# Leaky pass read from PSUM, weight requests on another queue, one conversion step later

## The chip, the cores and the metric

The kernel runs on one core of one Trainium2 chip. The metric is the device time of one execution in microseconds (us); the time before is 1096.64, the median of 3 runs (1096.25 to 1097.05). The engines are named as in the profile: PE multiplies matrices (PEld loads its weights), DVE is the vector engine, ACT the scalar engine, POOL is GpSimd, and SP issues DMAs. Each engine runs its instructions in order, and an instruction that waits holds up all behind it on its engine. "SPq" and "POOLq" are the DMA queues behind requests of SP and GpSimd.

## The reference

Three stages follow each other. First is attention over 4 images of 8 heads with 576 tokens of 64 values, in which every row keeps its 32 largest scores. Second is a dense mixture: 2304 tokens times 512 to 2048 to 512 with a leaky activation in the middle, one slope per hidden column. Third is a mixture of 8 experts, of which each token takes one, if a gate lets it in.

```python
scores = scale * np.matmul(q, k.transpose(0, 1, 3, 2))
kth = np.partition(scores, -32, axis=-1)[..., -32:-31]
scores = np.where(scores >= kth, scores, -1e9)          # then softmax, times v
x = attention.transpose(0, 2, 1, 3).reshape(2304, 512)
h = x @ w_in                                            # 512 -> 2048
g = np.maximum(h, 0.0) + alpha * np.minimum(h, 0.0)
x = g @ w_out                                           # 2048 -> 512
...
h = np.maximum(xc[mask] @ w1[e], 0.0)                   # e: largest gate logit
out[do_compute] = xc + gate_w * (h @ w2[e])
```

## The kernel before

Attention goes block by block: a step is one block of 128 query rows (the last has 64) for a pair of heads. In a step DVE finds the 32 largest scores of each row: a fold by maxima and minima (L438) makes shorter lists, and rounds of MAX8 and MATCH_REPLACE8 (L447, L450) take eight values at a time; L480 then masks the row of 577 scores, ACT takes the exponentials (L472), PE transposes (L510) and multiplies by the values (L543), and DVE scales the product px (L550).

Each step is written out as 14 slots. The table `STEP` says at which slot x each part of the steps around it is issued, and in each slot the planner (`slot`) also issues some of the waiting work of the first mixture, by a cost budget. So the order of instructions on each engine is the order of this program; no engine reorders.

The first mixture works on an image in two parts, of 256 and of 320 token columns; that makes 8 works, each with 16 units `up` (one per 128 hidden columns) and then the output products `down`. Seven of the works lie beside the attention of later steps, in what is called a stretch below; the eighth comes after the attention has ended, in the tail. The numbers are split into a high and a low part in place of full fp32 products, so that a unit has 12 matmuls (L614) into one PSUM bank `pm`, of which the pool has two. After it:

- one slot later, ACT reads the bank twice: relu(h) into `ra` (L625) and relu(-h) into `rb` (L626); the bank is free then (`read()`).
- after `LA` = 4 further slots the unit is ready for DVE's pass ra = -alpha * rb + ra (L638), but in a stretch that pass is held in a list `leaky` until slot 11 (`PH` + 2), so that DVE runs two to four of them just ahead of the next fold.
- ACT copies `ra` into the high part of `g` (L651), and GpSimd's subtraction (`sub`, L108) makes the low part. Late in a step `between` holds this back until slot 1 of the next, since the first GpSimd subtraction after a fold waits until the fold's last DVE pass is done (`gate`).

`need` and `fetch` ask for weights of the first mixture two chunks (1 MB each) ahead; `wload` (L558) puts a request on GpSimd's queue, into one of three buffers `wr`. There are 128 such requests. These weights are in a DRAM scratch: 32 conversions (`convert`) make them beside the first steps from the given weights, each with three ACT passes (L277 to L281), a DVE pass on the bit patterns (`bits`, L285), a split and a store.

SP's queue carries all other loads and stores, among them the value loads of the heads (L369), the rows of the first mixture's result (L764), and the expert weights `wraw` for the last stage (L992). In the tail, `splits` converts the latter on ACT (L998) and on other engines.

Of the kernel before, what the change touches and what calls it, by code (L numbers as in the profile page):

```python
# [7 lines left out]
F32 = mybir.dt.float32  # L8
# [38 lines left out]
LA = 4  # L47
# [11 lines left out]
def kernel(  # L59
# [44 lines left out]
    gate, now, held_back, leaky = [None], [None], [], []  # L104
# [83 lines left out]
    nalpha = const.tile([128, KF], F32, name="nalpha")  # L188
# [27 lines left out]
    def late_loads():  # L216
        nc.sync.dma_start(wg[:, :, :E], w_gate.rearrange("(d p) e -> p d e", p=128))
        nc.sync.dma_start(wg[:, :, E], w_skip.rearrange("(d p) -> p d", p=128))
        nc.sync.dma_start(nalpha, alpha.rearrange("(f p) -> p f", p=128))
# [47 lines left out]
    def convert(i):  # L267
# [37 lines left out]
        return none * (CV - 1) + [bits] + none * (CV - 1) + [split] + none * CV + [store]  # L305
# [274 lines left out]
    def moe1(xx, cols, x2t, base):  # L580
# [18 lines left out]
        hps, held = {}, [0, 0]  # L599

        def hf_of(f):
            return f // fs

        def up(wi, f, sg, half, first):
# [11 lines left out]
            if half == 0:  # L616
                return []
            ra = moe.tile([128, 320], F32, name="ra", tag="ra", bufs=6)[:, 0:n]
            rb = moe.tile([128, 320], F32, name="rb", tag="rb", bufs=4)[:, 0:n]
            held[0] += 1  # L620
            held[1] += 1
# [6 lines left out]
            soon = f >= (hf_of(f) + 1) * fs - 3  # L628

            def late2():  # L630
                if now[0] is None or now[0] > PH + 1 or soon:
                    late3()
                else:
                    leaky.append(late3)

            def late3():
                held[1] -= 1
                nc.vector.scalar_tensor_tensor(ra, rb, nalpha[:, f:f + 1], ra, op0=OP.mult, op1=OP.add)  # L638
                if soon:
                    late4()  # L640
                else:
                    between(late4)

            def late4():
                held[0] -= 1
# [4 lines left out]
                g[f, sg] = gt  # L650
                nc.scalar.activation(gt[:, 0, 0:n], ra, AF.Copy)  # L651
                sub(gt[:, 1, 0:n], ra, gt[:, 0, 0:n].bitcast(F32))
# [34 lines left out]
        for hf in range(nhf):  # L687
            for f in range(hf * fs, (hf + 1) * fs):
                for sg, (c0, c1) in enumerate(cols):
                    for half in range(2):  # L690
                        one = f % 2 == 0 and sg == 0 and half == 0
                        if half == 0:
                            parts.append((lambda: room() and held[0] < 6 and held[1] < 4, None))
# [423 lines left out]
    def main(work, exact, hooks=(lambda: [], lambda: [])):  # L1117
# [138 lines left out]
        for kx in range(-2, K + 2):  # L1256
# [21 lines left out]
            for x in range(NSLOT):  # L1278
# [3 lines left out]
                if x == PH + 2 or now[0] is None:  # L1282
                    late_leaky = leaky[:]
                    leaky.clear()
                else:
                    late_leaky = ()
# [14 lines left out]
                for f in late_leaky:  # L1301
                    f()
                slot(q if kx > -2 or exact else 0.65 if x in (0, 5, 6) else 0.0)
        now[0] = None
        release(leaky)
# [198 lines left out]
```

## Time and profile before

| what | value |
|---|---|
| time, median of 3 | 1096.64 us (1096.25 to 1097.05) |
| the profiled execution, its own time | 1101.48 us |
| its span in the trace | 1099.6 us |
| PE busy | 941.3 us, 86% |
| DVE busy | 938.3 us, 85% |
| ACT busy | 736.3 us, 67% |
| GpSimd busy | 503.5 us, 46% |
| GpSimd's DMA queue (q0) | 138.73 MB, 36.6% of 16 engines' span |
| SP's DMA queue (q1) | 113.62 MB, 32.7% |

A share of busy time is an average over stages with different limits. The rows below are therefore taken by stage: the start (0 to 30 us), the seven stretches (150 to 830), the tail of the first mixture (857 to 930) and the experts after it. The table of stretches lists the engines in the order PE, PEld, DVE, ACT, POOL. The idle time shown for an instruction is that of its engine just before it, with the line that ended it. Where two engines are near their limit, the order of the waits tells more than the busy shares: a wait that is short on one engine can be the one that another waits behind.

### The profile page before, as it was taken

What the parts mean: (1) busy time and instruction counts of PE and PEld (TensorE: products, weight loads), DVE (VectorE), ACT (ScalarE), POOL (GpSimd) and SP (SyncE); (2) the same over time, 40 slices, a digit from 0 to 9 for tenths busy, and PEclk for the clock granted to TensorE, in tenths of its full rate; (3) what the DMA queues carried; (4) which work ended last, traced back from release to release, by engine and by line L of the source; (5) the groups of instructions that cost most, each with busy time, mean ns of one, the idle gap of its engine ahead of it and who ended that gap; (6) DMA issues with size and microseconds to landing.
All of it is one profiled execution on the core that took longest, in us unless ns stands there. A gap on an engine that the chain in (4) does not pass through costs nothing.

```text
span 1099.6 us, 22163 instructions
## 1 busy us (share of the span) xinstructions
PE 941.3 (86%) x7270; PEld 852.3 (78%) x7270; DVE 938.3 (85%) x2943; ACT 736.3 (67%) x1932; POOL 503.5 (46%) x705
## 2 busy tenths in 40 slices
PE   4436659898999898999999899999889799799994
PEld 2235448798998797999988898999789798587883
DVE  4999998999999899899989998998994233899971
ACT  6869858765875685578567767865773352597870
POOL 4866665532662454346335533652452350327220
PEclk9966569998999998999999999999999899899998
DMA  7888985675575566676756577665557897799950
GB/s 229 283 273 213 307 245 184 192 237 171 195 245 189 162 211 220 225 227 207 236 186 189 200 246 221 223 229 181 174 195 243 302 344 261 274 353 396 348 218 14
DMA packets 154284, 254.15 MB, mean 231 GB/s; under 512 B 78062, under 2 KB 110830, under 8 KB 137776
## 3 DMA queue, kind: packets, MB, share of 16 engines
q0 software_dynamic: 20928, 138.73, 36.6%
q1 hardware_dynamic: 132032, 113.62, 32.7%
q8 instruction: 60, 0.98, 0.4%
q14 instruction: 64, 0.52, 0.1%
q10 hardware_dynamic: 1200, 0.30, 0.1%
HBM read 224.20 MB, written 29.71 MB: 231 GB/s over the span
## 4 chain that ended last, share of the span: by engine, by line
PE 45%; DVE 31%; ACT 8%; DMA 7%; issue 5%; POOL 4%; SPq 0%; POOLq 0%; ACTq 0%; DVEq 0%; another core or an unknown queue 0%
PE pm L669 14%; PE pm L614 7%; DVE v L447 6%; DVE F L438 4%; PE px L543 4%; DVE Ex L480 4%; PE px L1045 4%; PE pm L1027 4%; DVE m L438 3%; DVE F L450 3%; DVE ra L638 3%; PE ps L417 3%; PE pt L510 2%; DMA wr<-wout 2%; PE ps L343 1%
## 5 line engine op out<-in xcount | busy, mean ns | idle before, releaser
L614 PE MATMUL pm<-x,wr 128*128 128x256 f32 (+1 forms) x1536 | 246.3, 310 | 14.2 <-DMA wr<-win 6.3
L669 PE MATMUL pm<-g,wr 128*128 128x256 f32 (+1 forms) x1536 | 235.9, 303 | 6.4 <-DMA wr<-wout 6.3
L614 PEld LDWEIGHTS pm<-x,wr 128*128 128x128 f32 x1536 | 216.8, 195 | 21.6 <-issue 8.7
L669 PEld LDWEIGHTS pm<-g,wr 128*128 128x128 f32 x1536 | 210.0, 190 | 12.2 <-issue 4.2
L447 DVE MAX8 v<-F 128x8 f32<-128x72 f32 (+2 forms) x576 | 213.0, 405 | 1.1
L108 POOL TENSOR_TENSOR g<-ra,g 128x256 fp32r<-128x256 f32 (+1 forms) x128 | 108.9, 869 | 119.3 <-DVE st L485 49.6
L480 DVE SCALAR_TENSOR_TENSOR Ex<-sb,v,Ex 128x577 f32<-128x577 f32 x144 | 132.4, 949 | 0.0
L450 DVE MATCH_REPLACE8 F<-v,F 128x72 f32<-128x72 f32 (+1 forms) x432 | 122.9, 290 | 0.0
L422 ACT ACTIVATE sb<-ps 128x288 f32<-128x288 f32 x224 | 80.1, 416 | 63.9 <-PE ps L417 50.3
L472 ACT ACTIVATE Ex<-sb,st 128x576 f32<-128x576 f32 x144 | 105.7, 786 | 0.1
L522 ACT ACTIVATE PT<-pt 128x512 f32<-128x512 f32 x144 | 87.4, 608 | 14.2 <-PE pt L510 13.4
L638 DVE SCALAR_TENSOR_TENSOR ra<-rb,nalpha,ra 128x256 f32<-128x256 f32 (+1 forms) x128 | 71.3, 593 | 29.4 <-ACT rb L626 29.4
L625 ACT ACTIVATE ra<-pm 128x256 f32<-128x256 f32 (+1 forms) x128 | 53.6, 419 | 57.6 <-PE pm L614 55.2
L510 PE MATMUL pt<-ident,Ex 128*128 128x128 f32 x576 | 88.2, 285 | 4.5 <-ACT sb L422 4.3
L543 PE MATMUL px<-PT,vt 128*64 128x128 f32 (+1 forms) x1280 | 90.2, 288 | 0.0
L417 PE MATMUL ps<-kT,qT 64*128 64x288 f32 x576 | 81.2, 355 | 7.6 <-POOL kT L108 2.9
L108 POOL TENSOR_TENSOR x<-xf,x 128x128 fp32r<-128x128 f32 (+1 forms) x80 | 46.7, 584 | 72.0 <-ACT x L552 39.7
L417 PEld LDWEIGHTS ps<-kT,qT 64*128 64x128 f32 x576 | 63.2, 216 | 20.7 <-issue 9.4
L543 PEld LDWEIGHTS px<-PT,vt 128*64 128x64 f32 x1280 | 70.9, 149 | 9.9 <-issue 2.0
L510 PEld LDWEIGHTS pt<-ident,Ex 128*128 128x128 f32 x576 | 72.1, 148 | 7.1 <-ACT sb L422 6.9
L438 DVE TENSOR_TENSOR F<-m 128x144 f32<-128x144 f32 (+2 forms) x240 | 73.0, 356 | 0.0
L651 ACT ACTIVATE g<-ra 128x256 fp32r<-128x256 f32 (+1 forms) x128 | 51.0, 451 | 20.4 <-DVE ra L638 20.4
(434 smaller groups left out, 1975.9 us busy)
## 6 DMA issues: line engine op xcount, KB each, us to landing
wr<-win POOLq DMA_DIRECT2D x64, 1024.0 KB, 6.0
wr<-wout POOLq DMA_DIRECT2D x64, 1024.0 KB, 6.0
wraw<-in_moe_w_dram SPq DMA_DIRECT2D x88, 512.0 KB
wr<-in_moe_w_in_dram SPq DMA_DIRECT2D x16, 512.0 KB
vt<-in_v_dram SPq DMA_DIRECT2D x32, 256.0 KB
win<-cv SPq DMA_DIRECT2D x16, 512.0 KB
wr<-in_moe_w_out_dram SPq DMA_DIRECT2D x16, 512.0 KB
wout<-cv SPq DMA_DIRECT2D x32, 256.0 KB
```

The costliest lines, as they stand in the source:

```text
L108: i = nc.gpsimd.tensor_tensor(o, a, b, op=OP.subtract)
L417: nc.tensor.matmul(self.ps[h, j][:, 0:HALF], lhsT=hd["q"][gp, a, u * 128:(u + 1) * 128], rhs=hd["k"][gp, b_, c0:c0 + HALF], **se)
L438: gate[0] = nc.vector.tensor_tensor(o[:, n_], a[:, n_, 0:w], a[:, n_, w:2 * w], op=op)
L447: nc.vector.max(v8[:, h, r, :], F[:, h, 0:w])
L450: nc.vector.match_replace(out=F[:, h, 0:w], in_to_replace=v8[:, h, r, :], in_values=F[:, h, 0:w], imm_value=NEG)
L472: nc.scalar.activation(self.Ex[:, h, :], self.sb[:, h, :], AF.Exp, bias=self.st[:, 0, h:h + 1], scale=0.125)
L480: nc.vector.scalar_tensor_tensor(self.Exp[:, cs], self.sbp[:, cs], v8[:, h, 3, 7:8], self.Exp[:, cs], op0=OP.is_ge, op1=OP.mult, accum_out ...
L510: nc.tensor.transpose(pt[:, c * 128:(c + 1) * 128], P[:, c0:c0 + 128], ident)
L543: nc.tensor.matmul(x[h * 64:(h + 1) * 64, 0:n], lhsT=hd["vt"][:, h, c, :], rhs=rhs, start=False, stop=(c == SF - 1))
L614: nc.tensor.matmul(hp[:, 0:n], lhsT=w[:, (f % 2) * 8 + a * 4 + d, :], rhs=x[:, d, c0:c1], start=(i == 0), stop=(i == 3 * KD - 1))
L638: nc.vector.scalar_tensor_tensor(ra, rb, nalpha[:, f:f + 1], ra, op0=OP.mult, op1=OP.add)
L669: nc.tensor.matmul(op_[:, 0:n], lhsT=w[:, 2 * f + a, :], rhs=g[(hf + ch) * 8 + f, sg][:, gg, 0:n], start=(i == 0), stop=(i == ni - 1))
```

## The change

The unit's two relu passes become one, relu(-h) into `ra`; the buffer `rb` goes. DVE's pass takes its addend from the PSUM bank: ra = (1 - alpha) * ra + h, with `slope` = 1 - alpha prepared once in place of `nalpha`. The bank is therefore free only when DVE's pass is written (`read()` stands behind it). `LA` goes from 4 to 2, the list `leaky` with its slot 11 is dropped, so that DVE's pass stands wherever its slot comes, and ACT's copy of `g` is issued right behind it; only GpSimd's subtraction still goes through `between`. The limit of four units between relu and pass (`held[1]`) is gone.

`wload` issues its request on SP in place of GpSimd. Of the second conversion (i = 1) `bits` is queued 12 slots after its ACT passes in place of 3, and in the first step slots 3 and 4 get the budget that 5 and 6 had.

```diff
-LA = 4
+LA = 2
...
-        nc.vector.tensor_scalar(nalpha, nalpha, -1.0, None, op0=OP.mult)
+        nc.vector.tensor_scalar(slope, slope, -1.0, 1.0, op0=OP.mult, op1=OP.add)
...
-        return none * (CV - 1) + [bits] + none * (CV - 1) + [split] + none * CV + [store]
+        return none * (CV - 1 if i != 1 else 3 * CV) + [bits] + none * (CV - 1) + [split] + none * CV + [store]
...
-        nc.gpsimd.dma_start(t, src)
+        nc.sync.dma_start(t.bitcast(F32), src)
...
             def late1():
+                nc.scalar.activation(ra, hp[:, 0:n], AF.Relu, scale=-1.0)
+
+            def late2():
+                nc.vector.scalar_tensor_tensor(ra, ra, slope[:, f:f + 1], hp[:, 0:n], op0=OP.mult, op1=OP.add)
                 read()
-                nc.scalar.activation(ra, hp[:, 0:n], AF.Relu)
-                nc.scalar.activation(rb, hp[:, 0:n], AF.Relu, scale=-1.0)
...
-            def late2():
-                if now[0] is None or now[0] > PH + 1 or soon:
-                    late3()
-                else:
-                    leaky.append(late3)
-
-            def late3():
-                held[1] -= 1
-                nc.vector.scalar_tensor_tensor(ra, rb, nalpha[:, f:f + 1], ra, op0=OP.mult, op1=OP.add)
-                if soon:
-                    late4()
-                else:
-                    between(late4)
...
                 nc.scalar.activation(gt[:, 0, 0:n], ra, AF.Copy)
-                sub(gt[:, 1, 0:n], ra, gt[:, 0, 0:n].bitcast(F32))
+
+                def late3():
+                    held[0] -= 1
+                    g[f, sg] = gt
+                    sub(gt[:, 1, 0:n], ra, gt[:, 0, 0:n].bitcast(F32))
+
+                if soon:
+                    late3()
+                else:
+                    between(late3)
...
-                if x == PH + 2 or now[0] is None:
-                    late_leaky = leaky[:]
-                    leaky.clear()
...
-                slot(q if kx > -2 or exact else 0.65 if x in (0, 5, 6) else 0.0)
+                slot(q if kx > -2 or exact else 0.65 if x in (0, 3, 4) else 0.0)
```

The order on DVE at the end of the seventh stretch (815 to 823 us in the trace before) was this; `F` and `m` are the lists of the fold, `v` the values found, and L638 is the leaky pass, here three in one place.

```order
L550 TENSOR_TENSOR xf<-px,R 128x128
L447 MAX v_11879<-F 128x8 x2
L480 SCALAR_TENSOR_TENSOR Ex_145,st<-sb_141,v_11437,Ex_145 128x577
L638 SCALAR_TENSOR_TENSOR ra<-rb,nalpha,ra 128x256 x3
L438 TENSOR_TENSOR m<-sb_139 128x2x288
L438 TENSOR_TENSOR F<-sb_139 128x2x288
L438 TENSOR_TENSOR m<-m 128x2x144
L438 TENSOR_TENSOR F<-m 128x2x144
L438 TENSOR_TENSOR F<-m 128x2x72 x2
L485 RECIPROCAL st<-st 128x1
```

In the changed program the leaky pass has line L624 and reads `pm`, the PSUM bank; the same place on DVE is now:

```order
L550 TENSOR_TENSOR xf<-px,R 128x128
L447 MAX v_11669<-F 128x8 x2
L624 SCALAR_TENSOR_TENSOR ra<-ra,slope,pm 128x256
L480 SCALAR_TENSOR_TENSOR Ex_145,st<-sb_141,v_11243,Ex_145 128x577
L624 SCALAR_TENSOR_TENSOR ra<-ra,slope,pm 128x256
L438 TENSOR_TENSOR m<-sb_139 128x2x288
L438 TENSOR_TENSOR F<-sb_139 128x2x288
L438 TENSOR_TENSOR m<-m 128x2x144
L438 TENSOR_TENSOR F<-m 128x2x144
L438 TENSOR_TENSOR F<-m 128x2x72 x2
L624 SCALAR_TENSOR_TENSOR ra<-ra,slope,pm 128x256
L485 RECIPROCAL st<-st 128x1
```

The three passes ahead of the fold are single ones now: the first stands further up between two rounds (above this piece), the second ahead of L480, the third behind it. The one behind the fold is the next unit's, which stood a few rounds later before.

On SP's queue the tail of the first mixture began like this; L764 stores rows of the mixture's result, and L992 loads expert weights (each behind an instruction that sets no data, ISA).

```order
L764 DMA x2d<-xr 128x512
L764 DMA out_dram<-xr 128x512
L764 DMA x2d<-xr 128x512
L764 DMA out_dram<-xr 128x512
L992 ISA
L992 DMA wraw<-in_moe_w_dram 128x1024
L992 ISA
L992 DMA wraw<-in_moe_w_dram 128x1024
```

In the changed program the stores have line L752, the expert weights L980, and the weight requests of the first mixture (L558, `win` for the units, `wout` for the output products) stand in this queue:

```order
L752 DMA x2d<-xr 128x512
L752 DMA out_dram<-xr 128x512
L558 DMA wr<-win_125 128x2048
L558 DMA wr<-win_126 128x2048
L558 DMA wr<-win_127 128x2048
L558 DMA wr<-win_128 128x2048
L558 DMA wr<-win_129 128x2048
L558 DMA wr<-win_130 128x2048
L558 DMA wr<-wout_131 128x2048
L558 DMA wr<-wout_132 128x2048
L558 DMA wr<-wout_131 128x2048
L980 ISA
```

The first expert weight now stands behind six requests of input weights and three of output weights. The same six and three were on GpSimd's queue before.

## Rows read from the trace of the kernel before

**Rows 1.** Stretches: time, length, then busy us (instructions) by engine, PEclk, DMA share, GB/s.

```profile
150.00:830.00 680.00, 631.25 (x5517) 590.32 (x5517) 646.77 (x2317) 475.03 (x1437) 317.04 (x496) 0.97 0.64 207
...
857.00:897.00 40.00, 32.32 (x200) 31.18 (x200) 12.66 (x40) 18.18 (x48) 21.71 (x29) 0.91 0.94 326
```

**Rows 2.** Waits of DVE in 150 to 830 us: total us, times, longest.

```profile
DVE rc L779 <- ACT lg L744: 8.1, 3, 3.8
...
DVE rc L779 <- ACT lg L742: 5.9, 2, 3.3
DVE ra L638 <- ACT rb L626: 4.3, 3, 2.5
```

**Rows 3.** Forms on DVE: shape, count, busy us, mean ns, idle before.

```profile
L480 DVE SCALAR_TENSOR_TENSOR Ex<-sb,v,Ex 128x577 f32<-128x577 f32 x144 | 132.4, 949 | 0.0
...
L638 DVE SCALAR_TENSOR_TENSOR ra<-rb,nalpha,ra 128x320 f32<-128x320 f32 x64 | 38.2, 634 | 25.1 <-ACT rb L626 25.1
...
L638 DVE SCALAR_TENSOR_TENSOR ra<-rb,nalpha,ra 128x256 f32<-128x256 f32 x64 | 33.0, 553 | 4.3 <-ACT rb L626 4.3
...
L1053 DVE SCALAR_TENSOR_TENSOR orow<-px,ta,xg 128x512 f32<-128x512 f32 x8 | 5.9, 743 | 0.0
```

**Rows 4.** Two DVE lines by source: shortest, median, longest ns.

```profile
L638 DVE SCALAR_TENSOR_TENSOR ra<-rb,nalpha,ra x128: 473/540/1559, 164.1 to 899.9; 128x256 f32<-128x256 f32 x64, 128x320 f32<-128x320 f32 x64
...
L480 DVE SCALAR_TENSOR_TENSOR Ex<-sb,v,Ex x144: 795/815/2256, 37.5 to 836.4; 128x577 f32<-128x577 f32 x144
```

**Rows 5.** The page's groups: a relu pass on ACT.

```profile
L625 ACT ACTIVATE ra<-pm 128x256 f32<-128x256 f32 (+1 forms) x128 | 53.6, 419 | 57.6 <-PE pm L614 55.2
```

**Rows 6.** Timeline at 161 and 379 us: start, length, line, shape, idle before.

```profile
160.82 0.44 DVE L450 MATCH_REPLACE8 F<-v,F 128x288 f32<-128x288 f32 x1
...
164.99 0.38 ACT L625 ACTIVATE ra<-pm 128x256 f32<-128x256 f32 x1 [0.91 <-PE pm L614]
...
379.00 0.09 DVE L480 DVE_READ_ACCUMULATOR Ex<-sb,v,Ex 128x1 f32 x1
...
382.24 0.40 ACT L625 ACTIVATE ra<-pm 128x256 f32<-128x256 f32 x1
```

**Rows 7.** Timeline at 199 and 817 us, DVE and PE.

```profile
199.61 0.21 DVE L450 MATCH_REPLACE8 F<-v,F 128x72 f32<-128x72 f32 x1
...
199.75 0.95 PE L614 MATMUL pm<-x,wr 128*128 128x256 f32 x6
...
817.64 0.88 PE L669 MATMUL pm<-g,wr 128*128 128x256 f32 x6
...
817.84 0.08 DVE L480 DVE_READ_ACCUMULATOR Ex<-sb,v,Ex 128x1 f32 x1
```

**Rows 8.** A wait of ACT in 150 to 830 us.

```profile
ACT g L651 <- DVE ra L638: 16.4, 15, 2.4
```

**Rows 9.** Forms on GpSimd: a weight request, with the idle time before.

```profile
L558 POOL DMA_DIRECT2D wr<-win x64 | 36.6, 571 | 38.9 <-PE pm L669 14.9 <-DVE v L447 14.2 <-PE pm L614 5.5
```

**Rows 10.** Timeline of PE in the tail.

```profile
874.82 13.05 PE L614 MATMUL pm<-x,wr 128*128 128x320 f32 x72 [4.41 <-DMA wr<-win]
```

**Rows 11.** Chain of waits in the tail: start, us, what.

```profile
864.25 10.44 DMA wr<-win
...
904.27 7.58 DMA wr<-wout
```

**Rows 12.** Timeline of SP's queue in the tail.

```profile
860.31 43.26 SPq L992 DMA_DIRECT2D wraw<-in_moe_w_dram  x10
```

**Rows 13.** Timeline of ACT in the tail: first use of an expert weight.

```profile
897.70 1.06 ACT L998 ACTIVATE w1h<-wraw 128x1024 fp32r<-128x1024 f32 x1
```

**Rows 14.** Timeline of DVE at the start.

```profile
16.74 1.33 DVE L285 SCALAR_TENSOR_TENSOR cv<-cv 128x512 int32<-128x512 int32 x1 [6.31 <-ACT cv L281]
```

**Rows 15.** Timeline of ACT at the start.

```profile
28.24 0.67 ACT L277 ACTIVATE cv<-wr 128x512 f32<-128x512 f32 x1 [3.89 <-DMA wr<-in_moe_w_in_dram]
```

**Rows 16.** Waits of SP's queue in 150 to 830 us.

```profile
SPq L369 <- PE px L543: 336.4, 24, 22.8
```

More of the change, by code (lines that the diff above doesn't have):

```diff
@@ L102 @@
     ctx.enter_context(tc.manual_schedule())
-    gate, now, held_back, leaky = [None], [None], [], []
+    gate, now, held_back = [None], [None], []
     def sub(o, a, b):
@@ L187 @@
     wg = const.tile([128, KD, E + 1], F32, name="wg")
-    nalpha = const.tile([128, KF], F32, name="nalpha")
+    slope = const.tile([128, KF], F32, name="slope")
     cnt = const.tile([128, E], F32, name="cnt")
@@ L218, in late_loads @@
         nc.sync.dma_start(wg[:, :, E], w_skip.rearrange("(d p) -> p d", p=128))
-        nc.sync.dma_start(nalpha, alpha.rearrange("(f p) -> p f", p=128))
+        nc.sync.dma_start(slope, alpha.rearrange("(f p) -> p f", p=128))
         zeros = moe.tile([128, DM], F32, name="zeros", tag="xr", bufs=3)[:, 0:128]
@@ L597, in moe1 @@
         g = {}
-        hps, held = {}, [0, 0]
-        def hf_of(f):
-            return f // fs
+        hps, held = {}, [0]
         def up(wi, f, sg, half, first):
@@ L617, in up @@
                 return []
+            held[0] += 1
+            soon = f % fs >= fs - 3
             ra = moe.tile([128, 320], F32, name="ra", tag="ra", bufs=6)[:, 0:n]
-            rb = moe.tile([128, 320], F32, name="rb", tag="rb", bufs=4)[:, 0:n]
-            held[0] += 1
-            held[1] += 1
             def late1():
+                nc.scalar.activation(ra, hp[:, 0:n], AF.Relu, scale=-1.0)
+            def late2():
+                nc.vector.scalar_tensor_tensor(ra, ra, slope[:, f:f + 1], hp[:, 0:n], op0=OP.mult, op1=OP.add)
                 read()
-                nc.scalar.activation(ra, hp[:, 0:n], AF.Relu)
-                nc.scalar.activation(rb, hp[:, 0:n], AF.Relu, scale=-1.0)
-            soon = f >= (hf_of(f) + 1) * fs - 3
-            def late2():
-                if now[0] is None or now[0] > PH + 1 or soon:
-                    late3()
-                else:
-                    leaky.append(late3)
-            def late3():
-                held[1] -= 1
-                nc.vector.scalar_tensor_tensor(ra, rb, nalpha[:, f:f + 1], ra, op0=OP.mult, op1=OP.add)
-                if soon:
-                    late4()
-                else:
-                    between(late4)
-            def late4():
-                held[0] -= 1
                 key = ("p", f if nsg == 2 else f // 2)
@@ L649, in late4 @@
                 gt = g[key][:, sg if nsg == 2 else f % 2]
-                g[f, sg] = gt
                 nc.scalar.activation(gt[:, 0, 0:n], ra, AF.Copy)
-                sub(gt[:, 1, 0:n], ra, gt[:, 0, 0:n].bitcast(F32))
+                def late3():
[6 more added lines that the diff above has]
+                    between(late3)
             return [late1] + none * LA + [late2]
@@ L692, in moe1 @@
                         if half == 0:
-                            parts.append((lambda: room() and held[0] < 6 and held[1] < 4, None))
+                            parts.append((lambda: room() and held[0] < 6, None))
                         parts.append((6 * (c1 - c0) / 2400, lambda wi=wi, f=f, sg=sg, half=half, one=one:
@@ L1281, in main @@
                     release(held_back)
-                if x == PH + 2 or now[0] is None:
-                    late_leaky = leaky[:]
-                    leaky.clear()
-                else:
-                    late_leaky = ()
                 for at, d, name, *a in STEP:
@@ L1300, in main @@
                             queue_moe(steps[kx - 2][0])
-                for f in late_leaky:
-                    f()
-                slot(q if kx > -2 or exact else 0.65 if x in (0, 5, 6) else 0.0)
+                slot(q if kx > -2 or exact else 0.65 if x in (0, 3, 4) else 0.0)
         now[0] = None
-        release(leaky)
         release(held_back)
```

## The prediction

> **What bounds the kernel now.** I read the table of stretches first, to see how busy each engine is where the change acts. In 150 to 830 us, which holds seven stretches of 16 leaky units each, DVE is busy 646.8 of 680 us and PE 631.3: two engines share the pace, DVE a little ahead [rows 1]. The waits of DVE there come next: its largest are for the router's logits, 8.1 and 5.9 us in 5 waits; for the leaky pass it waits 4.3 us [rows 2]. DVE is held up about once per stretch and works through in between, so work taken off DVE inside a stretch should shorten it, and a new wait put on DVE should lengthen it. From 857 to 897 us DVE has little to do (12.7 of 40 us), PE is busy 32.3, and the DMA engines are at 0.94: that is the eighth work, which runs at the pace of its weight loads [rows 1]. So the change has three places: the seven stretches (112 units), the tail (16 units), and the program's start.
>
> **The change part by part.** All sums are against the profiled execution: 1101.48 us, span 1099.6. That is 4.84 above the median of 1096.64, and the same 4.84 is taken off at the end.
>
> (a) The leaky combination on DVE. The pass with two SBUF operands goes (128 of them: 553 ns at 256 columns, 634 at 320), and one with a PSUM operand comes in its place [rows 3]. No row shows that form at 256 or 320 columns; the nearest is L1053, whose first operand is PSUM, at 512 columns: 743 ns [rows 3]. What the same pass would take with SBUF operands at 512 I get from the fastest of L638 (473 at 256) and of L480 (795 at 577) [rows 4]: (795 - 473) / 321 = 1.003 ns per column, so 473 + 256 x 1.003 = 730. PSUM then costs 13 ns more, and the new pass takes 486 and 550. The saving is 67 ns at 256 and 84 ns at 320. All of it is stalls: the means of L638 stand 80 and 97 ns above its fastest (473, and 473 + 64 x 1.003 = 537), with one pass at 1559 ns [rows 3, 4]. I take it that these passes stand beside GpSimd work and that a pass with one SBUF operand escapes this. Outside the tail there are 64 passes of 256 and 48 of 320 columns: 64 x 67 + 48 x 84 = 8.3 us. Bounds: at most 12 us (the 16 tail passes, and some delay of the instruction behind, too), at least nothing: the stalls move to the neighbours, of which L480 has 154 ns on the mean over its fastest, 144 x 154 = 22 us [rows 3, 4]. I take -8.3.
>
> [...]
>
> (b) One of two relu passes on ACT goes, 128 x 419 ns = 53.6 us of ACT's time [rows 5]. ACT does not set the pace; what shows on the path is L638's wait for the second relu, 4.3 us in the stretches [rows 2], of 25.1 + 4.3 over the program [rows 3]; the rest lies in the tail, where PE sets the pace. Bounds 0 and -4.3; I take -1.0, since the new pass waits for the one relu that stays.
>
> (c) The new waits. Before, DVE ran these passes in a bunch just ahead of the next fold, long after the relus. Now each stands between two selection rounds, two slots behind its relu, and DVE issues in order: all later rounds queue behind a pass that waits. I laid the new place of each pass against the times of before. The worst is in the first stretch: DVE would come to the place at 160.82 + 0.44 = 161.3, ACT has the relu at 164.99 + 0.38 = 165.4, so 4.1 us of waiting. In the third stretch DVE is there at 379.1 and the relu is done 382.24 + 0.40 = 382.6, and ACT can't do it sooner than its own place allows, so 3.6 [rows 6]. Once DVE is late by that much it does not wait again for anything less late, so a stretch pays its largest, not the sum; and what DVE waits at the logits, 14.0 / 5 = 2.8 us each [rows 2], covers it wherever the logits come after. I count the first in full, 4.1, the third with 3.6 - 2.8 = 0.8, and 0.6 for the other five together: +5.5. Bounds 0 (all covered) and +15 (nothing covered: 4.1 + 3.6 and about 1.5 for each other).
>
> ACT's copy g is now queued at once behind each pass and ACT can stand there, with the softmax's exponentials and the fold's input copies behind it. It waits for DVE at this place already, 16.4 us in 15 waits [rows 8]. These few waits become many short ones; ACT has 205 us of slack in the 680. I take +2, bounds 0 and +7.
>
> The PSUM bank of a unit is freed by DVE now and by ACT before, so PE's next use of it can come too early. I compared the end of each new pass with the moment at which PE took that bank before. In 30 of the 112 places it would be late, by 0.1 to 1.8 us and 21 us in sum. The first over 0.2 us: DVE gets there at 199.82, so the pass is done about 200.3, and PE took the bank at 199.75. The last: DVE there at 817.9, done 818.4, PE took the bank at 817.64 [rows 7]. PE, though, was at these moments ahead of DVE, and would only wait earlier for what it waits for anyway. I take 0, bounds 0 and +21.
>
> (d) The weight requests. 128 requests leave GpSimd's queue, 64 of them 36.6 us with idle time of 38.9 in front, the other 64 alike [rows 9]; that frees GpSimd for the low parts of g. In the seven stretches the loads are early enough to cost PE next to nothing, so only the tail counts. There PE stands 4.41 us ahead of a unit at 874.82 for a chunk that was requested at 864.25, behind a subtraction, and took 10.44 us [rows 10, 11], while ten expert-weight loads had been put on SP's queue from 860.31 on [rows 12]. In the new order six weight requests stand before the first of those, so this wait should go: -4.4, and a part of the idle 7.7 of 40 us elsewhere. Against it, the expert weights now queue behind the third output chunk, about 897, and ACT wanted the first at 897.70 [rows 13]; the tail has no DMA time to spare (0.94), so I give back most of what I gain on the output chunks (7.58 us for one [rows 11]). I take -3, bounds -10 and +8.
>
> (e) The start. The second conversion's bits go behind the first fold, which had to wait until they were done at 16.74 + 1.33 = 18.1; DVE had been idle 6.31 us before them [rows 14]. Bounds 0 and -6.3. But ACT still stands until 28.24 for a weight load, with the first exponentials behind it [rows 15], so most of the gain is waited away again: -1.5.
>
> Sum: -8.3 - 1.0 + 5.5 + 2 - 3 - 1.5 = -6.3. 1101.48 - 6.3 = 1095.2 in a profiled execution, less 4.84: 1090.3, rounded to 1090.
>
> **The rivals.**
>
> R1, slower: the bank. PE runs ahead, and stands at the bank each time DVE is late with a pass, for 21 us [rows 7]; DVE then waits less for PE's units, so +5.5 drops out: -6.3 + 21 - 5.5 = +9.2, 1105.8. For it: PE is nearly as busy as DVE, and a late unit delays the matmuls of the heads in order behind it. Against it: no such wait was there before, and DVE gets a little faster. It decides from 6.3 + 5.5 = 11.8 us of such waits on. Chance 0.23.
>
> R2, no change: DVE's waits for the relu are paid in every stretch. With 4.1 and 3.6 and 0.8 more in each of five, term (c) is 11.7 and not 5.5, and the sum is -0.1: 1096.5. For it: the waits stand on the busiest engine. Against it: the logits' cover. Chance 0.14.
>
> R3, slower: SP's queue. Its value loads wait for PE 24 times, 336.4 us together and up to 22.8 each, with all requests behind them in order [rows 16]; or the expert weights come late in the tail. Term (d) at +8 gives -6.3 + 11 = +4.7: 1101.3. Against it: a value load waits for PE work that comes earlier in the program than the chunk's last use. Chance 0.04.
>
> R4, no change: a PSUM operand costs DVE as much as the stalls it avoids, (a) is nothing: +2.0, 1098.6. For it: one row of 743 ns is all there is, and it is for another size. [...] Chance 0.05.
>
> **How the numbers follow.** The forecast has 0.54. About 0.2%, or 2.2 us, is what a measurement of this kernel can tell from no change: 1094.4 to 1098.8. The forecast's own range, with (c) from 0 to about 10 and (a) from -12 to -4, is 1078 to 1095; nearly all of it is faster (0.51, 0.03 same). R2 and R4 lie mostly inside the band (0.12 same, 0.05 faster, 0.02 slower), R1 and R3 above it (0.27). Faster 0.56, same 0.15, slower 0.29. The range takes in R1's time and goes down to (a), (d) and (e) near their better bounds: 1076 to 1107.
>
> **What would show it.** (a): the new pass at about 490 and 550 ns on the mean, and no growth in the mean of the pass with 577 columns. (c): waits of DVE's new pass for ACT's relu, once or twice a stretch, some 5 to 10 us in all; a wait of PE's unit for that pass at the bank of more than 12 us would prove R1. (d): PE's wait of 4.41 us in the tail gone, first use of the expert weights later than 897.7. (e): the first fold ahead of 18 us and the exponentials still near 30. The forecast is wrong if DVE's idle time in the seven stretches grows by more than its busy time falls.

## The result and the profile after

The changed kernel takes 1085.72 us (median of 6 runs, 1084.09 to 1090.57), the kernel before 1096.85 in the same runs. The ratio is 0.9911 (95% interval 0.9890 to 0.9932): 9.8 us faster. The forecast was 1090, with 6.3 us to be gained. The direction, the range and roughly the size are right. The sum behind them is not, as the experiments show: its leaky part is some 5 us too good and its queue term some 10 us too small. That these two errors cancel in part is luck.

The profiled execution fell by 16.9 us, from 1101.48 to 1084.56. That is more than the ratio says, because the first trace of before was of a long execution (4.84 us above its median) and that of the changed kernel of a slightly short one (1.16 below). A second trace of the kernel before stands further down; it is of a short execution.

The table of stretches of the changed kernel, in the columns of [rows 1]:

```profile
150.00:830.00 680.00, 638.48 (x5596) 594.67 (x5597) 638.58 (x2333) 448.36 (x1330) 256.46 (x390) 0.98 0.63 209
857.00:897.00 40.00, 38.40 (x259) 37.70 (x258) 13.26 (x19) 17.33 (x35) 14.99 (x18) 1.00 0.91 348
```

DVE is busy 638.6 of 680 us while the program is further on at the end of this window, and ACT's load fell by 27 us. In the window of the tail PE now works 38.4 of 40 us instead of 32.3, at a granted clock (PEclk) of 1.00 instead of 0.91. The forms of the passes on DVE, with their mean in ns and the idle time before them:

```profile
L480 DVE SCALAR_TENSOR_TENSOR Ex<-sb,v,Ex 128x577 f32<-128x577 f32 x144 | 129.8, 928 | 0.0
...
L624 DVE SCALAR_TENSOR_TENSOR ra<-ra,slope,pm 128x320 f32<-128x320 f32 x64 | 34.5, 539 | 22.9 <-ACT ra L621 22.1 <-POOL kT L108 0.4 <-POOL qbd L108 0.3
...
L624 DVE SCALAR_TENSOR_TENSOR ra<-ra,slope,pm 128x256 f32<-128x256 f32 x64 | 30.1, 470 | 9.3 <-ACT ra L621 8.1 <-POOL qbd L108 0.9
```

And its line by source, shortest, median and longest:

```profile
L624 DVE SCALAR_TENSOR_TENSOR ra<-ra,slope,pm x128: 453/502/549, 158.5 to 880.3; 128x256 f32<-128x256 f32 x64, 128x320 f32<-128x320 f32 x64
```

The new pass takes 470 and 539 ns against 553 and 634 [rows 3], and the 1559 ns of the longest [rows 4] is 549 now: no pass is held up for long any more. The waits of DVE in 150 to 830 us, to be read against [rows 2]:

```profile
DVE ra L624 <- ACT ra L621: 12.1, 15, 2.7
DVE rc L767 <- ACT lg L732: 8.3, 3, 3.8
DVE rc L767 <- ACT lg L730: 5.3, 2, 2.7
```

The waits at the logits are as they were, 13.6 us; the leaky pass waits for its relu 12.1 us in 15 places, where it waited 4.3 in 3. The waits of PE in the same window, first before and then after:

```profile
PE px L512 <- DVE xf L550: 10.3, 10, 3.1
PE px L539 <- ACT R L528: 9.0, 6, 1.9
PE ps L343 <- ACT sb L422: 7.2, 7, 1.8
PE px L515 <- DVE xf L550: 5.6, 5, 2.3
```

```profile
PE pm L611 <- DVE ra L624: 10.3, 18, 1.4
PE px L512 <- DVE xf L550: 8.8, 9, 3.0
PE px L539 <- ACT R L528: 7.6, 6, 1.8
PE px L515 <- DVE xf L550: 3.1, 4, 1.0
...
PE ps L343 <- ACT sb L422: 1.3, 2, 0.9
...
PE pm L802 <- DVE ra L624: 1.2, 2, 0.8
...
PE pm L657 <- DVE ra L624: 0.5, 1, 0.5
```

PE now waits for the bank that DVE frees, 10.3 us in 18 places, 12.0 with the two small rows at the end. The other four fell together from 32.1 to 20.8 us; in the trace of the requests alone (first experiment), which has the same queue and the old pass, they are 31.1. So by its size the bank's wait took the place of waits that PE had anyway.

ACT's wait at the copy g answers to [rows 8]: 67.5 us in 81 waits, where it was 16.4 in 15.

```profile
ACT g L630 <- DVE ra L624: 67.5, 81, 2.9
```

In the tail, PE's timeline after, with the idle time in brackets, answers to [rows 10], and SP's queue to [rows 12]:

```profile
858.37 21.36 PE L611 MATMUL pm<-x,wr 128*128 128x320 f32 x144 [0.25 <-DMA wr<-win]
...
895.39 7.56 PE L657 MATMUL pm<-g,wr 128*128 128x320 f32 x48 [1.36 <-DMA wr<-wout]
905.09 8.84 PE L657 MATMUL pm<-g,wr 128*128 128x320 f32 x48 [2.14 <-DMA wr<-wout]
```

```profile
851.74 17.79 SPq L558 DMA_DIRECT2D wr<-win  x6
872.72 7.36 SPq L558 DMA_DIRECT2D wr<-wout  x3
880.30 0.90 SPq L980 DMA_DIRECT2D wraw<-in_moe_w_dram  x2
```

```profile
886.28 1.06 ACT L986 ACTIVATE w1h<-wraw 128x1024 fp32r<-128x1024 f32 x1 [4.94 <-DMA wraw<-in_moe_w_dram]
```

Twelve of the tail's 16 units, 144 matmuls, run through with 0.25 us of waiting in front, in place of 4.41 us. The expert weights go out from 880.30 on, behind nine requests, and ACT, free for the first of them, waits 4.94 us for it (third fence). Between the output products PE waits 1.36 and 2.14 us.

At the start, the first fold's pass (DVE) and the load that ACT waits for, against [rows 14, 15]:

```profile
10.79 0.76 DVE L438 TENSOR_TENSOR m<-sb 128x576 f32<-128x576 f32 x1 [0.75 <-ACT sb L422]
```

```profile
27.60 0.67 ACT L277 ACTIVATE cv<-wr 128x512 f32<-128x512 f32 x1 [3.25 <-DMA wr<-in_moe_w_in_dram]
```

The fold starts at 10.79, some 7 us earlier, and ACT still stands until 27.60 where it stood until 28.24: 0.6 us of the 7 is left.

### The profile page after: what moved, and what is told of

Its sections match the earlier page's. It is cut to its first block, busy times and chain, and to the rows that moved or that the text cites. A ratio compares the mean times of both kernels' runs of the same rounds, so it can differ in the third digit from the quotient of the medians.

```text
span 1082.8 us, 21930 instructions
## 1 busy us (share of the span) xinstructions
PE 935.1 (86%) x7270; PEld 844.8 (78%) x7270; DVE 922.2 (85%) x2943; ACT 703.0 (65%) x1804; POOL 429.7 (40%) x577
## 4 chain that ended last, share of the span: by engine, by line
PE 41%; DVE 37%; issue 6%; ACT 6%; POOL 5%; DMA 5%; SPq 0%; POOLq 0%; DVEq 0%; ACTq 0%
PE pm L657 14%; DVE v L447 8%; PE pm L611 6%; DVE F L438 5%; DVE Ex L480 5%; DVE m L438 4%; DVE F L450 4%; PE px L1033 4%; PE pm L1015 4%; PE px L543 4%; DVE ra L624 3%; PE ps L417 2%; PE pt L510 2%; POOL cv L108 2%; PE pm L723 1%
## 5 line engine op out<-in xcount | busy, mean ns | idle before, releaser
L611 PE MATMUL pm<-x,wr 128*128 128x256 f32 (+1 forms) x1536 | 248.8, 309 | 17.0 <-DVE ra L624 10.3
L108 POOL TENSOR_TENSOR g<-ra,g 128x256 fp32r<-128x256 f32 (+1 forms) x128 | 104.9, 824 | 185.8 <-ACT g L630 95.6
L480 DVE SCALAR_TENSOR_TENSOR Ex<-sb,v,Ex 128x577 f32<-128x577 f32 x144 | 129.8, 928 | 0.0
L630 ACT ACTIVATE g<-ra 128x256 fp32r<-128x256 f32 (+1 forms) x128 | 57.1, 446 | 75.1 <-DVE ra L624 73.3
L624 DVE SCALAR_TENSOR_TENSOR ra<-ra,slope,pm 128x256 f32<-128x256 f32 (+1 forms) x128 | 64.6, 505 | 32.1 <-ACT ra L621 30.2
L510 PE MATMUL pt<-ident,Ex 128*128 128x128 f32 x576 | 85.9, 281 | 2.6 <-ACT sb L422 2.6
L108 POOL TENSOR_TENSOR x<-xf,x 128x128 fp32r<-128x128 f32 (+1 forms) x80 | 49.3, 617 | 96.0 <-ACT x L552 94.8
L438 DVE TENSOR_TENSOR F<-m 128x144 f32<-128x144 f32 (+2 forms) x240 | 70.2, 344 | 0.0
```

Of the source, the lines that this page charges most:

```text
L108: i = nc.gpsimd.tensor_tensor(o, a, b, op=OP.subtract)
L438: gate[0] = nc.vector.tensor_tensor(o[:, n_], a[:, n_, 0:w], a[:, n_, w:2 * w], op=op)
L480: nc.vector.scalar_tensor_tensor(self.Exp[:, cs], self.sbp[:, cs], v8[:, h, 3, 7:8], self.Exp[:, cs], op0=OP.is_ge, op1=OP.mult, accum_out ...
L510: nc.tensor.transpose(pt[:, c * 128:(c + 1) * 128], P[:, c0:c0 + 128], ident)
L611: nc.tensor.matmul(hp[:, 0:n], lhsT=w[:, (f % 2) * 8 + a * 4 + d, :], rhs=x[:, d, c0:c1], start=(i == 0), stop=(i == 3 * KD - 1))
L624: nc.vector.scalar_tensor_tensor(ra, ra, slope[:, f:f + 1], hp[:, 0:n], op0=OP.mult, op1=OP.add)
```

## The experiments

Each was timed beside the kernel before on the same chip, in several rounds; a ratio is to that kernel, with its 95% interval. One per cent is 11 us. The changed kernel has 0.9911 (0.9890 to 0.9932) from the first comparison and 0.9922 (0.9894 to 0.9949) from the second below.

**The requests alone.**

```diff
 (the kernel before)
-        nc.gpsimd.dma_start(t, src)
+        nc.sync.dma_start(t.bitcast(F32), src)
```

> The kernel before, with the first mixture's weight requests on SP's queue as the only edit. Theory T (the requests matter in the tail alone): the wait of 4.41 us ahead of the unit at 874.8 goes, the units of the tail end some 8 us earlier, the output products give about 3 back, the seven stretches stay within 1 us: about 5 us faster, 1091 to 1093. Rival Q (GpSimd, free of 72 us of requests, makes the low parts of g sooner in the stretches): the stretches shorten by 4 us or more as well, 1088 or less. Rival N (the tail's gain in the changed kernel came from DVE's pass, not from the queue): within 2 us of before.

0.9877 (0.9857 to 0.9898): 13.5 us faster, all that the whole change brings and more. Theory T, which is the prediction's, had 5 us; rival Q is nearer. In its trace PE, ACT and DVE in the tail show a new place that costs something:

```profile
889.38 0.64 PE L669 MATMUL pm<-g,wr 128*128 128x320 f32 x1 [3.71 <-ACT g L651]
```

```profile
886.05 1.06 ACT L998 ACTIVATE w1h<-wraw 128x1024 fp32r<-128x1024 f32 x1 [6.18 <-DMA wraw<-in_moe_w_dram]
888.86 0.47 ACT L651 ACTIVATE g<-ra 128x320 fp32r<-128x320 f32 x1 [1.75 <-DVE ra L638]
```

```profile
887.14 1.23 DVE L999 TENSOR_TENSOR w1h<-wraw,w1h 128x1024 fp32r<-128x1024 f32 x1 [8.73 <-ACT w1h L998]
888.28 0.55 DVE L638 SCALAR_TENSOR_TENSOR ra<-rb,nalpha,ra 128x320 f32<-128x320 f32 x1
```

ACT waits 6.18 us for the first expert weight. On DVE the last leaky pass of the units is queued behind a pass on that same weight (L999), and on ACT the last copy g waits for this pass, 1.75 us more. PE waits 3.71 us for the copy. In the changed kernel pass and copy stand ahead of the weight.

**The requests back on GpSimd.**

```diff
 (the changed kernel)
-        nc.sync.dma_start(t.bitcast(F32), src)
+        nc.gpsimd.dma_start(t, src)
```

> The changed kernel with the requests back on GpSimd's queue. Theory T: the tail is as before (units wait for a chunk some 4 us once, 8 us lost in all, 3 won back), the stretches keep their gain of about 8 us: 1088 to 1091. Rival Q: the stretches lose 4 us or more against the changed kernel. Rival N: within 2 us of the changed kernel.

1.0048 (1.0032 to 1.0063): 5.3 us slower than before. The leaky part and the start together, without the queue, are a loss. Theory T fails here: no gain of the stretches is left. Its waits in 150 to 830 us, of DVE and of PE:

```profile
DVE ra L624 <- ACT ra L621: 13.9, 13, 3.4
```

```profile
PE pm L611 <- DVE ra L624: 10.4, 17, 1.4
```

They are those of the changed kernel (12.1 and 10.3), so they belong to the leaky part and not to the queue.

**The start as before.**

```diff
 (the changed kernel)
-        return none * (CV - 1 if i != 1 else 3 * CV) + [bits] + ...
+        return none * (CV - 1) + [bits] + ...
...
-                slot(q if kx > -2 or exact else 0.65 if x in (0, 3, 4) else 0.0)
+                slot(q if kx > -2 or exact else 0.65 if x in (0, 5, 6) else 0.0)
```

> The changed kernel with the second conversion's bits and the slots of the first step as before. Theory T: the first pass with 577 columns comes at 37.5 again and not at 36.8, and all after it is later by this: +0.7 us, not to be told from the changed kernel by its time. Rival S (what the first fold wins is kept further on): +3 us or more.

0.9912 (0.9895 to 0.9929), that of the changed kernel in the other two comparisons. The first pass with 577 columns began at 38.8 us against 36.8. The start is worth too little to be told by the time; the 3 us or more of rival S are not seen.

**The new order with the old pass.** DVE's order is that of the changed kernel, row by row, but the pass reads two SBUF operands and waits for the second of two relus.

```diff
 (the changed kernel)
-                nc.scalar.activation(ra, hp[:, 0:n], AF.Relu, scale=-1.0)
+                nc.scalar.activation(ra, hp[:, 0:n], AF.Relu)
+                nc.scalar.activation(rb, hp[:, 0:n], AF.Relu, scale=-1.0)
...
-                nc.vector.scalar_tensor_tensor(ra, ra, slope[:, f:f + 1], hp[:, 0:n], op0=OP.mult, op1=OP.add)
+                nc.vector.scalar_tensor_tensor(ra, rb, slope[:, f:f + 1], ra, op0=OP.mult, op1=OP.add)
```

(`slope` holds -alpha here.)

> The changed kernel in the same order on DVE, but with two relu passes on ACT and DVE's pass on two SBUF operands, so that PE waits for ACT and not for DVE at the bank. Theory T (the stalls of 80 to 97 ns belong to the two SBUF operands, and PE's 12 us at the bank are waits it would have elsewhere): the pass takes about 550 and 630 ns again on the mean, PE's waits at the bank for DVE go, others take their place, and the kernel is 6 to 10 us slower than the changed one. Rival P (the stalls belonged to the place ahead of the fold): the pass takes 480 and 545 ns here too, and the time is that of the changed kernel or lower. Rival R1 (the bank costs its 12 us in full): 5 us or more faster than the changed kernel, whatever the pass takes.

1.0061 (1.0046 to 1.0076), 15 to 16 us slower than the changed kernel: the sign of theory T, and twice its size. R1's 5 us or more of gain are not there: with PE freed from DVE at the bank nothing got faster. The edit also adds a relu, so it does not price the bank alone. The pass by form, and DVE's wait for the relu in 150 to 830 us:

```profile
L626 DVE SCALAR_TENSOR_TENSOR ra<-rb,slope,ra 128x320 f32<-128x320 f32 x64 | 38.8, 606 | 22.5 <-ACT rb L623 21.4 <-POOL kT L353 1.1
...
L626 DVE SCALAR_TENSOR_TENSOR ra<-rb,slope,ra 128x256 f32<-128x256 f32 x64 | 32.2, 503 | 18.1 <-ACT rb L623 18.1
```

```profile
DVE ra L626 <- ACT rb L623: 21.3, 23, 3.1
```

In the new place the old pass takes 503 and 606 ns. In the eight traces with the old place its means run from 517 to 560 and from 610 to 650 ns (553 and 634 in the first trace of before); the new pass has 470 to 473 and 539 to 541 in five. So by these means the two SBUF operands are worth 30 to 33 ns at 256 columns and 65 to 67 at 320, the place 14 to 57 and 4 to 44, and P, which had 480 and 545, falls. Only the longest pass is clearly shorter in the new place: 887 ns, against 1154 to 1660. The larger item is the wait, 21.3 us where it is 12.1 with one relu. The following rows have DVE's account: the stretch from the 17th pass with 577 columns to the last (columns as in [rows 1]), of the requests alone, of the changed kernel, and of this one.

```profile
144.00:827.30 683.30, 639.15 (x5619) 597.14 (x5620) 652.79 (x2350) 483.35 (x1456) 266.81 (x394) 0.97 0.64 210
```

```profile
143.10:827.90 684.80, 642.32 (x5620) 597.44 (x5621) 644.40 (x2351) 453.89 (x1343) 261.12 (x394) 0.97 0.63 210
```

```profile
142.90:844.60 701.70, 644.74 (x5619) 596.57 (x5620) 650.90 (x2351) 482.20 (x1456) 262.04 (x394) 0.97 0.62 205
```

From the first to the second, DVE is busy 8.4 us less (652.8 to 644.4) and idle 9.9 more (30.5 to 40.4). Against two other traces with the old pass and the requests on SP (last table of this section) it is busy 3 to 5 us less and idle 11 more. The leaky part saves something on DVE, up to what it promised, and gives back more in waits. From the second to the third, idle time grows by 10.4 and busy time by 6.5: the 16.9 us between them. So one relu in place of two, which I had put down at 1 us, is worth some ten times that as soon as DVE stands right behind it.

**The changed kernel again, and the requests with the start.** The second kernel is the one before with SP's queue and the start's two lines, and the old leaky part.

> The changed kernel itself once more, beside the next ones on one chip. What the two first comparisons said (0.9911 for it, 0.9877 for the requests alone) should stay: 0.990 to 0.992 of before.

> The kernel before with the requests on SP's queue and the start of the changed kernel (bits behind the first fold, slots 3 and 4), and the leaky part as it was. Theory L (the leaky part gives back all that it saves): 2 to 5 us faster than the changed kernel. Rival G (the leaky part is a gain that the requests alone can't reach): slower than the changed kernel, 1088 or more.

0.9922 (0.9894 to 0.9949) and 0.9903 (0.9869 to 0.9936). Theory L has the sign, 2 us, but these two intervals overlap, and alone they would not settle it. With the requests alone at 0.9877 against 0.9912 for the changed kernel with the old start (one chip, intervals that touch), and with 1.0048 on the other queue (there with the start), each of three comparisons puts the leaky part at a loss of 2 to 5 us; only the last of them is clear of noise.

**The request waits its turn on GpSimd again.** Both kernels are the one with the requests alone, and GpSimd writes a part of the buffer ahead of each request.

```diff
 (the requests alone)
+        nc.gpsimd.memset(t[0:1, 0, 0:1].bitcast(F32), 0.0)
         nc.sync.dma_start(t.bitcast(F32), src)
...
 (the second kernel)
+        nc.gpsimd.memset(t[0:1, 0:4, :].bitcast(F32), 0.0)
         nc.sync.dma_start(t.bitcast(F32), src)
```

> The kernel before with the requests on SP, but ahead of each one GpSimd writes one element of the buffer, so that the request waits again until GpSimd's queue has come to it, without GpSimd's 0.57 us for the request. Theory W (a request was late because it stood behind GpSimd's waiting subtractions): the stretches lose most of the 9 us that the move had won them, PE waits some 4 us for output weights near 430 to 445 again, the tail's units lose 4 to 8 us: 3 us or less faster than before. Rival C (it was GpSimd's time for the requests, 72 us, and what DVE loses beside it): the gain of the requests alone stays, 1085 to 1088.

> As the kernel with one written element, but GpSimd writes 512 elements of one partition of the buffer ahead of each request, so that it is also busy about as long as with the request itself (0.5 us, by estimate from the 0.57 us of a request). Theory W: within 2 us of the kernel with one element. Rival C: 5 us or more slower than that one, near the time of before.

0.9960 (0.9936 to 0.9984) and 1.0028 (1.0008 to 1.0047). The writes on GpSimd, by form:

```profile
L558 POOL MEMSET wr<- 1x1 f32 x128 | 11.3, 88 | 78.2 <-issue 34.3 <-PE pm L670 30.8 <-PE pm L615 11.7
```

```profile
L558 POOL MEMSET wr<- 1x512 f32 x128 | 66.0, 516 | 74.8 <-PE pm L670 32.2 <-issue 29.8 <-PE pm L615 10.5
```

With 88 ns of work, waiting for GpSimd's turn costs more than half of the gain: 6 of 11 us against the requests with the start on the same chip (0.9903), 9 of 13.5 against the requests alone on another. With 516 ns, close to the 571 of a request [rows 9], some 7 us more go, and the kernel is 3 us slower than before. By the times both theories hold a part: the turn, and GpSimd's time. The place where W expected the loss was wrong, though: of the 4 us that PE should wait for output weights near 430 to 445 us, one trace has 1.2 and the other nothing, and the last pass with 577 columns comes at 825.2 and 828.2 us, as early as with the requests alone (827.3). The loss shows behind that pass, where the rest of the program takes 266.8 and 267.0 us, against 260.1 with the requests alone and 263.2 before. These edits do more than give back the old order: all of SP's queue, with the expert weights in it, now waits for GpSimd too. In 150 to 830 us of the first:

```profile
SPq L559 <- POOL wr L558: 353.1, 88, 11.1
```

So they show that the kernel pays for GpSimd's turn and time, but not that the requests paid for them in this way in the kernel before.

**Before, a second look.**

> The kernel before, for a second profiled execution, since the first stood 4.84 us above the median. If the first was long by chance, the last pass with 577 columns comes near 831 us and not 836.4, and PE does not wait for output weights at 431 and near 450. If the waits belong to the kernel, both come again.

1095.33 us, span 1093.5. The last pass with 577 columns, of the first trace and of the second:

```profile
836.45 0.81 DVE L480 SCALAR_TENSOR_TENSOR Ex<-sb,v,Ex 128x577 f32<-128x577 f32 x1
```

```profile
829.06 0.81 DVE L480 SCALAR_TENSOR_TENSOR Ex<-sb,v,Ex 128x577 f32<-128x577 f32 x1
```

The same program reaches this point 7.4 us earlier, and PE waits for no output weights in 150 to 830 us (4.3 us in the first). The first trace was long by chance; this one is short by chance, 4.2 us under the median of the 17 executions timed beside it (1099.5). So the 8.6 us by which the changed kernel's trace is ahead of the first at this point are 1.2 against the second, and a usual execution lies between. A single trace of this kernel can't say where the 13.5 us go.

**Only the tail's requests.**

```diff
 (the kernel before; wload is given the number j of the request)
+        if j < 7 * 16:
             nc.gpsimd.dma_start(t, src)
+        else:
+            nc.sync.dma_start(t.bitcast(F32), src)
```

> The kernel before, with only the 16 requests of the eighth work on SP's queue, the other 112 on GpSimd as before. Theory T of the prediction (only the tail counts): as fast as with all requests moved, 0.986 to 0.990 of before. Rival Q (the stretches hold the larger share): 0.994 to 0.997, some 5 us of the 12.

0.9985 (0.9971 to 1.0000): 1.6 us. The other 112 requests are worth about 12 (0.9985 - 0.9877 = 0.0108, from two chips). The prediction's claim that only the tail counts falls, more plainly than rival Q had it.

**One slot later.**

```diff
 (the changed kernel)
-LA = 2
+LA = 3
```

> The changed kernel with DVE's leaky pass one slot later (LA = 3). Theory M (the pass is caught between ACT's relu ahead of it and PE's need of the bank behind it, so a shift only trades one for the other): DVE's waits for the relu fall from 12 us to 6 or less, PE's waits at the bank rise from 12 to 16 or more, and the time stays within 3 us of the changed kernel. Rival D (DVE's waits for the relu alone set the price): 5 us or more faster.

0.9912 (0.9894 to 0.9931), that of the changed kernel. The waits in 150 to 830 us, of DVE and of PE:

```profile
DVE rc L767 <- ACT lg L732: 11.2, 3, 6.7
DVE ra L624 <- ACT ra L621: 8.0, 6, 2.1
```

```profile
PE pm L611 <- DVE ra L624: 12.4, 18, 1.5
```

Both numbers of theory M missed (8.0 and not under 6; at the bank 13.2 with a small row, and not over 16), but what they were for held: 4.1 us less of one wait, 1.2 more at the bank and 2.9 more at the logits, and no time gained. Rival D falls.

**A version with what paid.** The requests and the start, and in the tail the pass two slots behind its relu, so that the last copy g comes ahead of the expert weight:

```diff
 (the kernel with the requests and the start)
-            return [late1] + none * LA + [late2]
+            return [late1] + none * (LA if now[0] is not None else 2) + [late2]
```

> The kernel before with the requests on SP and the start of the changed kernel, and with the leaky pass two slots after its relu in the tail alone, so that the last copy g stands ahead of the first expert weight on ACT (with the requests alone PE waited 3.7 us there). Theory L: 2 to 4 us faster than the one without this edit, 0.986 to 0.988 of before, and faster than the changed kernel by 3 us or more. Rival G: no faster than the changed kernel.

0.9880 (0.9857 to 0.9904), 1084.89 us in its runs. PE's timeline at the same place:

```profile
873.92 14.27 PE L669 MATMUL pm<-g,wr 128*128 128x320 f32 x96
889.55 7.53 PE L669 MATMUL pm<-g,wr 128*128 128x320 f32 x48 [1.36 <-DMA wr<-wout]
```

The 3.71 us are gone: 96 matmuls run through. By the ratios it is 3 to 5 us ahead of the changed kernel, with intervals that overlap a little. From the requests alone it can't be told, nor from the requests with the start (0.9903, 2.5 us behind, on another chip), so theory L is not shown by the time.

**The traces side by side.** The table has, from one trace each, the stretch from the 17th pass with 577 columns to the last, DVE's busy and idle time in it, and what the program takes from there to its end. "Old" and "new" are the leaky part.

| kernel | requests | leaky part | stretch, us | DVE busy | DVE idle | rest, us |
|---|---|---|---|---|---|---|
| before | GpSimd | old | 692.6 | 658.2 | 34.4 | 263.2 |
| before, second look | GpSimd | old | 685.0 | 655.7 | 29.3 | 264.4 |
| only the tail's requests | GpSimd, tail SP | old | 689.7 | 654.7 | 35.0 | 258.8 |
| the requests alone | SP | old | 683.3 | 652.8 | 30.5 | 260.1 |
| the requests with the start | SP | old | 676.6 | 647.5 | 29.1 | 260.0 |
| what paid | SP | old, its pass earlier in the tail | 679.5 | 649.8 | 29.7 | 255.0 |
| changed | SP | new | 684.8 | 644.4 | 40.4 | 254.9 |
| changed, again | SP | new | 684.7 | 644.9 | 39.8 | 258.6 |
| the start as before | SP | new | 689.4 | 643.5 | 45.9 | 255.1 |
| the requests back | GpSimd | new | 693.5 | 648.7 | 44.8 | 264.0 |

The rows of the kernels with the old pass, the first three with the requests of the stretches on GpSimd and the last two with all on SP (columns as in [rows 1]):

```profile
143.80:836.40 692.60, 643.79 (x5619) 601.41 (x5620) 658.17 (x2350) 483.34 (x1455) 323.93 (x504) 0.97 0.64 207
144.10:829.10 685.00, 638.77 (x5620) 595.75 (x5620) 655.71 (x2351) 482.98 (x1456) 324.65 (x504) 0.97 0.65 210
144.10:833.80 689.70, 642.82 (x5620) 600.25 (x5621) 654.74 (x2351) 482.89 (x1455) 324.70 (x504) 0.97 0.64 208
143.50:820.10 676.60, 635.06 (x5619) 594.50 (x5620) 647.47 (x2351) 482.62 (x1455) 272.26 (x394) 0.98 0.64 213
142.70:822.20 679.50, 637.18 (x5619) 596.51 (x5620) 649.80 (x2350) 482.89 (x1455) 272.28 (x394) 0.98 0.64 212
```

Single traces of one kernel differ by up to 7.6 us in the stretch and 3.7 in the rest, so only the pattern counts. Taking the requests off GpSimd shortens the stretch by some 9 us (means 689.1 and 679.8), of which 6 are DVE's busy time for the same instructions, and the rest by 4. The new leaky part makes the stretch longer: with the requests on SP, DVE is busy 6 us less and idle 12 more. In the rest it wins back up to 5 us, and so does the one edit to the tail of the kernel with what paid. A part of the last column is PE's clock: the two traces of the changed kernel have 225.9 and 230.1 us of busy time for the same 1279 matmuls there, at a granted clock of 0.96 and 0.94.

## Why the prediction came out right, step by step

(a) DVE's pass: the direction was right, and the size nearly. I forecast 486 and 550 ns, and 470 and 539 were measured, which makes 64 x 83 + 48 x 95 = 9.9 us over the means of before. In DVE's account the difference was 8.4 from one trace to one other and 6 on the mean of three and three, and the forecast 8.3: right, or a little too large. The stalls did not move to the neighbours: the pass with 577 columns has 928 ns after 949. That is the queue's doing and not the leaky part's, since the requests alone have 928 too and the requests back on GpSimd 961. PSUM cost nothing extra in this form: the shortest new pass is 453 ns against 473 with SBUF operands [rows 4], and R4 falls.

(b) and (c), the waits: this is the first step that failed. The relu that goes (b) was put at 1.0 us as a matter of ACT's path; the kernel with two relus in the new order shows that it is worth 9 to 10 us of DVE's waits, but only because the pass now stands right behind it. I had "a stretch pays its largest, not the sum", and let the waits at the logits cover all but the first stretch: 5.5 us, plus 2 for ACT. Measured are, with one relu left, 12.1 us in 15 places, in six of the seven stretches and several times in most of them, and 10 to 12 us more idle time of DVE. The waits at the logits did not shrink (14.0 to 13.6). So a stretch pays the sum, and the cover that I had assumed was not there; why being late by a relu does not shorten the wait at the logits is not shown. Thus (a) + (b) + (c), forecast at -1.8, is +2 to +5. The prediction had named the sign of this itself: it is wrong if DVE's idle time in the stretches grows by more than its busy time falls, and that is what happened. It is R2 that came true for the leaky part, by the mechanism it named. What the forecast left out is the rest of the program, where the new order wins some of it back.

The bank (R1): PE's waits there, 12.0 us, came to the point at which I had said that R1 decides. It did not decide: PE's other waits fell by 11.3, or by 10.3 from the requests alone, and the kernel in which PE does not wait for DVE there is no faster. That fits the reason that I gave, that PE would only wait earlier for what it waits for anyway. No run frees the bank and changes nothing else, so the reason is not shown.

(d) The requests: the second step that failed, and the one that made the sum come out. "Only the tail counts" and -3 were read from a table in which the loads cost PE next to nothing in the stretches. The tail is worth 1.6 us, the other 112 requests about 12. Of the tail's details the 4.41 us went as forecast and ACT waits for the expert weight, but the first use of it came at 886.28, not later than 897.7. What I had left unpriced in the sum is what the requests cost in the stretches: 72 us of GpSimd's time, the order on GpSimd, behind which both the loads and the low parts of g stand, and some 6 us of DVE's own busy time in the table. I had written that moving them "frees GpSimd for the low parts of g", and given it no term.

(e) The start: -1.5 was forecast, 0.6 is in the trace, nothing in the time. The reason named for it, ACT's load at 28, fits: ACT stands until 27.60 for it.

Together: 4 to 7 us too good on DVE's side, about 10 too bad on the queue's. R3 fell: with the requests behind the value loads in SP's queue, PE waits for no weight chunk in 150 to 820 us.

What stays open is by what mechanism the requests on GpSimd cost their 12 us in the stretches. By the table some 6 us of it are DVE passes that take longer, the pass with 577 columns among them; the rest are waits that I could not name, since the two traces of before differ by 7.4 us at the end of the stretches. The two kernels with GpSimd's writes lose their time behind the stretches and do not settle it. Several traces of each kernel would be wanted.

## What to carry to other kernels

When an engine's pass is moved from a bunch to right behind its producer, price the wait for the producer at every place, and take off for cover only waits that stand for the same engine and end by the same event. Price an issuing engine's queue as a resource even where the engine is half idle: 128 requests of 0.57 us at 46% load cost more than everything that was saved on the busiest engine. And take a second trace of the kernel before, if the first lies away from its median; the second can lie away on the other side, as here.

## What the runs showed of the hardware

- A request of 1 MB takes GpSimd 571 ns [rows 9] and lands 6.0 us after issue; from SP's queue the median was 4.9.
- A DVE pass with two SBUF operands had a longest of 1559 ns [rows 4]; with one operand from PSUM, and the requests on GpSimd as before (the requests back), the longest of 128 was 549 too.
- The DVE pass with 577 columns took 949 to 961 ns on the mean in the four traces with the stretches' requests on GpSimd, and 914 to 941 in the ten with all on SP. With GpSimd writing for 516 ns ahead of each request on SP it took 929, so GpSimd's busy time alone does not make the difference.
